# Chunked state-space scan and bilinear feed-forward on one core: one late store moved to GpSimd's queue, the state-decay spread as two 64-column products, two filler products fewer

## The chip, the cores and the metric

The kernel runs on one core of one Trainium2 chip. The metric is device time in microseconds (us), the median of several executions, lower is better. The profile is one further execution, recorded by the hardware profiler. PE is TensorE (matrix products; PEld are its weight loads), DVE is VectorE, ACT is ScalarE, POOL is GpSimd, SP is SyncE, which here only issues DMAs.

## The reference, cut to what matters

Two operators follow each other. The first is a chunked state-space scan over 4 batches, 8 heads and 768 steps, with head size 32 and state size 16:

```
cum = cumsum(log a)                      # within a chunk
M[i,j] = (C_i . B_j) * exp(cum_i - cum_j)   for i >= j
y[i]   = sum_j M[i,j] x_j  +  exp(cum_i) * C_i . state
state  = exp(sum log a) * state + sum_j exp(cum_last - cum_j) B_j x_j
```

The heads of `y` are then put side by side (3072 tokens of width 256) and go through the second operator, `((y @ w_a) * (y @ w_b)) @ w_out` with `d_ff` = 1536. Inputs and output are float32.

## The kernel before, in words

Sequences are cut into 6 blocks of 128 steps (`NBLK`), and the 4 batches into 2 pairs (`NBP`), which makes 12 pairs `p` of (block, two batches). For a pair the kernel scales B and C by running decays (`scale_bc`), turns them (on PE with `transposes` for the first four pairs, by a DMA transpose, `turn`, for the others), multiplies them (`scores`, into the PSUM tiles `SC`), multiplies by the causal mask (`mask`, mostly on DVE, at times on ACT and POOL), scales x (`scale_x`, L287 when on ACT), and forms y (`pv` with `pv_u`, L433; `outputs` for later pairs). The per-block decay of the state, one number for each head and block, is computed by POOL on 32 partitions (`hsx`, L795), spread to 128 partitions by a product with an indicator matrix (`gps`, L815), and copied by ACT to `G` (L818); `state_sums` multiplies by it.

The feed-forward part takes y in units. A unit is one "up" product pair, `aps` with `Wa` and `bps` with `Wb` (L601 for the first four pairs, `unit_mm`; L667 for blocks, `bunit`), an ACT copy of `aps` (`asb`, L615) and a DVE product with `bps` (L622 or L679). `out_mm` (L637) and `bout` (L694) multiply by `Wo`, ACT or DVE scales the result into `osb` (L706, L704), and a DMA stores it. `bout(blk, c, parts)` does a block's quarter `c`; the last one, `bout(5, 3, 2)`, is done in two halves, one stored from SP's queue and one from ACT's.

The order of the work on each engine is written out by hand: the kernel runs under a manual schedule, and each engine executes its instructions in the order of the program. Semaphore waits are put in by the framework. PSUM work tiles come from four banks, taken in the order of a written-out string (`BANKS`); a new tile in a bank waits until the last reader of the old tile is done. By that string `gps` has the bank of an `aps` tile, and the decay-factor tile behind it (`fps`, made by `factors(3, NBLK, ...)`, L248) has the bank of the tile `bps` of unit (1, 1), whose reader is DVE's product L622.

Two things at the edges matter here. Early on, PE has filler products (`warmup(n, bank)`, L220, on a zeroed tile) between real work; those at L775 stand behind the transposes of pair 1 and ahead of the first up products:

```
transposes(1, apart=True)
...
warmup(2, tcp)
aps = [unit_mm(0, 0, Wa), unit_mm(0, 1, Wa)]
asb = [evac_a(aps[0])]
scores(1)
```

And at the end, the DMAs of SP and ACT take turns on eight completion semaphores, in program order over both queues, and those of POOL on eight others. SP closes the program with a row of records (L1039) in which it waits for each of the sixteen, two at a time, from the first hardware one to the eighth, and then enters the barrier of all engines.

Of the kernel before, what the change touches and what calls it, by code (L numbers as in the profile page):

```python
# [28 lines left out]
def kernel(  # L29
# [13 lines left out]
    nc = tc.nc  # L43

    nb, H, S, D = x.shape
    N = B.shape[-1]
    Q = 128
    NBLK = S // Q
# [7 lines left out]
    NG = NBLK - 1  # L56
# [21 lines left out]
    indm = c32[:, 0:128]  # L78
# [26 lines left out]
    hsx = big.tile([BH, nb, NG], f32, name="hsx")  # L105
# [21 lines left out]
    def bank(name):  # L127
        return psf.tile([128, 512], f32, name=name, tag=f"ff{next(banks)}")
# [89 lines left out]
    def warmup(n, bank, cols=512):  # L218
        for _ in range(n):
            nc.tensor.matmul(  # L220
                bank[:, 0:cols], warm[:, 0:128], warm[:, 0:cols], start=True, stop=True, skip_group_check=True
            )
# [9 lines left out]
    def sel_over_mid(lo, hi, eng):  # L232
        eng.tensor_tensor(
            out=selr[:, lo:hi].rearrange("p k t c -> p k (t c)"),
            in0=sel.rearrange("p t b h -> p (t b h)").unsqueeze(1).broadcast_to((BH, hi - lo, 2 * NBP * H)),
            in1=rmid[:, lo:hi].unsqueeze(2).broadcast_to((BH, hi - lo, 2 * NBP * H)),
            op=ALU.mult,
        )
# [357 lines left out]
    def unit_mm(p, k2, W):  # L596
        ps = bank("aps" if W is Wa else "bps")
        for kk in range(2):
            k = 2 * k2 + kk
            for f in range(2):  # L600
                nc.tensor.matmul(  # L601
                    ps[:, kk * 2 * Q : (kk + 1) * 2 * Q],
                    W[k // 6][:, f, k % 6 // 3 * 384 : (k % 6 // 3 + 1) * 384].rearrange("p (c kk) -> p kk c", kk=3)[
                        :, k % 3
                    ],
                    X2T[:, p, :, f],
                    start=(f == 0),
                    stop=(f == 1),
                    skip_group_check=True,
                )  # L610
        return ps
# [73 lines left out]
    def bout(blk, c, parts=1):  # L685
        bt, j = divmod(c, NBP)
        hk = st[("FF", blk)]["hk"]
        rows = out[(2 * j + bt) * S + blk * Q :][0:Q]
        w = d_model // parts
        for part in range(parts):  # L690
            o_ps = bank("ops")
            cs = slice(part * w, part * w + w)
            for k in range(NK):
                nc.tensor.matmul(  # L694
                    o_ps[:, 0:w],
                    hk[:, k, c * Q : (c + 1) * Q],
                    Wo[:, k, cs],
                    start=(k == 0),
                    stop=(k == NK - 1),
                    skip_group_check=True,  # L700
                )
            o_sb = outp.tile([128, d_model], f32, name="osb", tag="osb")
            if parts > 1 and part == 0:
                nc.vector.tensor_scalar(o_sb[:, 0:w], o_ps[:, 0:w], 1.0 / (YS * YS), None, ALU.mult)  # L704
            else:
                nc.scalar.activation(out=o_sb[:, 0:w], in_=o_ps[:, 0:w], func=AF.Copy, scale=1.0 / (YS * YS))  # L706
            (nc.sync, nc.scalar)[part].dma_start(rows[:, cs], o_sb[:, 0:w])

    def loads_bc(p):
        if p < NP:  # L710
# [31 lines left out]
    tb, tcp = bank("tb"), bank("tc")  # L742
# [29 lines left out]
    scan(5, NBLK)  # L772
    over_mid(1, NBLK)
    sel_over_mid(1, NBLK, nc.vector)
    warmup(2, tcp)  # L775
    aps = [unit_mm(0, 0, Wa), unit_mm(0, 1, Wa)]
    asb = [evac_a(aps[0])]
    scores(1)
# [29 lines left out]
    for k2 in range(1, 3):  # L808
# [3 lines left out]
    scale_bc(2, 1, nc.gpsimd)  # L812
    go((1, 0), (1, 1), (1, 2))
    gps = bank("gps")
    nc.tensor.matmul(  # L815
        gps[:, 0 : nb * NG], indm, hsx.rearrange("p b g -> p (b g)"), start=True, stop=True, skip_group_check=True
    )
    nc.scalar.copy(G.rearrange("p b g -> p (b g)"), gps[:, 0 : nb * NG])  # L818
    factors(3, NBLK, bank("fps"))
    state_sums(0)  # L820
# [149 lines left out]
    masked(7, (0, 1, 2), *bu(2, 5, 6, 7, 8, 9, 10, 11))  # L970
    group(3)
    bout(2, 0)
    bout(2, 1)

    stage(8, True, (6, 7))
# [7 lines left out]
    for blk in range(4, NBLK):  # L983
        pB = blk * NBP + 1
        stage(pB, False)
        if blk > 4:
            prep_x(pB)
        loads_x(pB + 2, nc.sync)
        prep(pB + 2)
        masked(pB, (0, 1))  # L990
        bout(blk - 2, 2)
        masked(pB, (2, 3), *bu(blk - 1, 6, 7, 8, 9))
        group(blk)
        bout(blk - 2, 3)
        bgo(blk - 1, 10, 11)
        if blk + 1 < NBLK:
            stage(pB + 1, False, (pB - 1, pB))
            prep_x(pB + 1)
            masked(pB + 1, (0, 1))
            bout(blk - 1, 0)  # L1000
            masked(pB + 1, (2,))
            bout(blk - 1, 1)
            masked(pB + 1, (3,), *bu(blk, 0, 1, 2, 3, 4, 5))
# [40 lines left out]
```

## Time and profile before

| what | value |
|---|---|
| runs (3) | 124.07, 124.44, 124.65 us; median 124.44 us |
| the profiled execution's own time | 123.91 us |
| its span (first to last instruction) | 122.2 us |
| busy share: PE, DVE, ACT, POOL | 96%, 70%, 58%, 51% |
| the chain that ended last, by engine | PE 93%, ACT 1%, POOL 1%, DVE 1% |
| granted TensorE clock | 1.0 |

The span is the time between the first and the last recorded instruction; what lies around it is 1.7 us in this execution. Busy shares are averages over the span. The chain of work that ended last is followed back from the last instruction; a line on it is work that nothing else hid, as far as the profile shows.

### The profile page before, as it was taken

How to read it: one execution, taken by the hardware profiler on the slowest of the kernel's cores; microseconds unless marked ns; L12 is line 12 of the kernel's file. 1: busy time of each engine (PE TensorE's matmuls, PEld its weight loads, DVE VectorE, ACT ScalarE, POOL GpSimd, SP SyncE). 2: the span in 40 equal slices, each digit the busy share in tenths (PEclk: the TensorE clock that was granted, in tenths of full speed). 3: DMA queues.
4: the chain of work that ended last, by engine and by line, in shares of the span. 5: the costliest groups of instructions: out<-in, count | busy, mean ns of one | idle time of the engine just before them, and what ended most of it. 6: DMA issues, size and time to landing. Idle time of an engine off the chain costs nothing.

```text
span 122.2 us, 3713 instructions
## 1 busy us (share of the span) xinstructions
PE 117.1 (96%) x1455; PEld 80.1 (66%) x1455; DVE 85.9 (70%) x163; ACT 71.4 (58%) x141; POOL 61.9 (51%) x107
## 2 busy tenths in 40 slices
PE   5999999999999999999999999999999999999990
PEld 2446789978898898644476464766465684645880
DVE  1877897795969599499984999667799435748000
ACT  0367756866466477887668637745645737575230
POOL 7999998966953876099921993147400000000000
PEclk9999999999999999999999999999999999999999
DMA  3999999998969999799789854879501012010131
GB/s 64 165 167 240 152 215 155 218 143 83 95 95 131 150 104 155 76 134 148 55 143 128 200 187 127 96 102 160 161 0 51 16 45 68 0 48 0 43 117 55
DMA packets 66737, 13.73 MB, mean 112 GB/s; under 512 B 61616, under 2 KB 66384, under 8 KB 66720
## 3 DMA queue, kind: packets, MB, share of 16 engines
q1 hardware_dynamic: 62592, 9.53, 49.8%
q0 software_dynamic: 2128, 3.61, 16.8%
q10 hardware_dynamic: 2000, 0.36, 1.6%
q8 instruction: 11, 0.18, 0.7%
q14 instruction: 6, 0.05, 0.1%
HBM read 11.13 MB, written 3.15 MB: 117 GB/s over the span
## 4 chain that ended last, share of the span: by engine, by line
PE 93%; ACT 1%; issue 1%; POOL 1%; DVE 1%; POOLq 0%
PE ops L694 18%; PE aps L667 17%; PE bps L667 17%; PE aps L601 9%; PE ops L637 9%; PE bps L601 9%; PE SC L220 3%; PE SC L358 2%; PE SC L419 2%; PE SC L373 1%; PE SC L433 1%; PE SC L508 1%; PE fps L260 1%; POOL bm L304 1%; ACT bt L337 1%
## 5 line engine op out<-in xcount | busy, mean ns | idle before, releaser
L615 ACT COPY asb<-aps 128x512 f32<-128x512 f32 x72 | 42.0, 586 | 14.3 <-PE aps L667 9.6
L679 DVE TENSOR_TENSOR hkb<-bps,asb 128x512 f16<-128x512 f32 x48 | 32.4, 689 | 12.6 <-ACT asb L615 11.4
L667 PE MATMUL aps<-XB,Wa 128*128 128x512 f16 x96 | 28.6, 379 | 0.0
L667 PE MATMUL bps<-XB,Wb 128*128 128x512 f16 x96 | 28.5, 379 | 0.0
L694 PE MATMUL ops<-Wo,hkb 128*128 128x256 f16 (+1 forms) x204 | 22.5, 267 | 0.0
L694 PEld LDWEIGHTS <-hkb 128*128 128x128 f16 x204 | 18.5, 98 | 3.1
L413 DVE TENSOR_TENSOR t<-SC,causal_q 128x512 f16<-128x512 f32 x27 | 17.3, 682 | 3.3 <-PE SC L358 3.3
L622 DVE TENSOR_TENSOR hk<-bps,asb 128x512 f16<-128x512 f32 x24 | 16.2, 684 | 4.1 <-ACT asb L615 3.7
L667 PEld LDWEIGHTS <-Wb 128*128 128x128 f16 x96 | 9.9, 103 | 10.9
L667 PEld LDWEIGHTS <-Wa 128*128 128x128 f16 x96 | 9.7, 103 | 9.1 <-issue 0.2
L601 PE MATMUL aps<-X2T,Wa 128*128 128x256 f16 x96 | 14.3, 274 | 0.2 <-DVE X2T L493 0.2
L706 ACT ACTIVATE osb<-ops 128x256 f32<-128x256 f32 (+1 forms) x16 | 6.0, 377 | 14.3 <-PE ops L694 14.2
L601 PE MATMUL bps<-X2T,Wb 128*128 128x256 f16 x96 | 14.1, 273 | 0.0
L411 POOL TENSOR_TENSOR t<-tmp,causal_q 128x512 f16<-128x512 f32 x5 | 5.8, 1161 | 11.7 <-ACT tmp L410 11.6
L289 POOL TENSOR_SCALAR x<-xn 128x512 f16<-128x512 f32 x7 | 10.4, 1490 | 2.1 <-DMA xn<-in_x_dram 1.8
L637 PE MATMUL ops<-Wo,hk 128*128 128x256 f16 x96 | 11.3, 273 | 0.0
L601 PEld LDWEIGHTS <-Wa 128*128 128x128 f16 x96 | 9.4, 103 | 1.3 <-DVE X2T L493 0.3
L601 PEld LDWEIGHTS <-Wb 128*128 128x128 f16 x96 | 9.8, 103 | 0.6
L637 PEld LDWEIGHTS <-hk 128*128 128x128 f16 x96 | 9.0, 98 | 1.3
L413 DVE TENSOR_TENSOR t<-SC,causal 128x512 f16<-128x512 f32 x13 | 8.2, 684 | 0.9 <-PE SC L373 0.8
L304 POOL TENSOR_TENSOR bm<-bn,fB 128x256 f16<-128x256 f32 x11 | 7.1, 642 | 2.5 <-DMA bn<-in_B_dram 1.7
L296 POOL TENSOR_TENSOR planes<-cn,fC 128x256 f16<-128x256 f32 x8 | 5.0, 620 | 4.7 <-DMA cn<-in_C_dram 4.5
(94 smaller groups left out, 117.0 us busy)
## 6 DMA issues: line engine op xcount, KB each, us to landing
out_dram<-osb SPq DMA_DIRECT2D x23, 128.0 KB, 1.8
xn<-in_x_dram SPq DMA_DIRECT2D x7, 256.0 KB, 4.2
cn<-in_C_dram SPq DMA_DIRECT2D x8, 128.0 KB, 3.9
bn<-in_B_dram SPq DMA_DIRECT2D x8, 128.0 KB, 4.5
Wa<-in_moe_w_a_dram POOLq DMA_DIRECT2D x2, 384.0 KB, 5.9
Wb<-in_moe_w_b_dram POOLq DMA_DIRECT2D x2, 384.0 KB, 7.3
Wo<-in_moe_w_out_dram POOLq DMA_DIRECT2D x2, 384.0 KB, 6.7
xn<-in_x_dram POOLq DMA_DIRECT2D x4, 128.0 KB, 6.5
```

What stands on the lines that cost most here:

```text
L289: eng.tensor_scalar(xo, xi, XS, None, ALU.mult)
L304: eng.tensor_tensor(out=m_, in0=raw, in1=(f[:, blk, :, bp] if factor is None else factor).unsqueeze(3).broadcast_to((128, 2, H, N)), op=AL ...
L411: nc.gpsimd.tensor_tensor(out=o_, in0=tmp, in1=c_, op=ALU.mult)
L413: nc.vector.tensor_tensor(out=o_, in0=i_, in1=c_, op=ALU.mult)
L601: nc.tensor.matmul(ps[:, kk * 2 * Q : (kk + 1) * 2 * Q], W[k // 6][:, f, k % 6 // 3 * 384 : (k % 6 // 3 + 1) * 384].rearrange("p (c kk) -> ...
L615: (nc.vector.tensor_copy if on_dve else nc.scalar.copy)(asb, a_ps)
L622: nc.vector.tensor_tensor(out=s["hk"][:, 2 * k2 : 2 * k2 + 2, :].rearrange("p k q -> p (k q)"), in0=b_ps, in1=asb, op=ALU.mult)
L637: nc.tensor.matmul(o_ps[:, 0:d_model], hk[:, k, bt * Q : (bt + 1) * Q], Wo[:, k, :], start=(k == 0), stop=(k == NK - 1), skip_group_check= ...
L667: nc.tensor.matmul(t_, W[k // 6][:, f, k % 6 // 3 * 384 : (k % 6 // 3 + 1) * 384].rearrange("p (c kk) -> p kk c", kk=3)[:, k % 3], XB[:, b ...
L679: return lambda: nc.vector.tensor_tensor(out=s["hk"][:, k], in0=ps[1], in1=asb, op=ALU.mult)
L694: nc.tensor.matmul(o_ps[:, 0:w], hk[:, k, c * Q : (c + 1) * Q], Wo[:, k, cs], start=(k == 0), stop=(k == NK - 1), skip_group_check=True,)
L706: nc.scalar.activation(out=o_sb[:, 0:w], in_=o_ps[:, 0:w], func=AF.Copy, scale=1.0 / (YS * YS))
```

## The change

Three edits. The store of `bout(4, 3)` is issued from GpSimd's queue instead of SP's. The spread of the state decays is written as two products of 64 columns each (the two halves of the array's columns) instead of one of 128. The two fillers at L775 are left out.

```diff
-            (nc.sync, nc.scalar)[part].dma_start(rows[:, cs], o_sb[:, 0:w])
+            eng = nc.gpsimd if (blk, c) == (NBLK - 2, 3) else (nc.sync, nc.scalar)[part]
+            eng.dma_start(rows[:, cs], o_sb[:, 0:w])
...
     sel_over_mid(1, NBLK, nc.vector)
-    warmup(2, tcp)
     aps = [unit_mm(0, 0, Wa), unit_mm(0, 1, Wa)]
...
     gps = bank("gps")
-    nc.tensor.matmul(
-        gps[:, 0 : nb * NG], indm, hsx.rearrange("p b g -> p (b g)"), start=True, stop=True, skip_group_check=True
-    )
+    for c0 in (0, 64):
+        nc.tensor.matmul(
+            gps[c0 : c0 + 64, 0 : nb * NG],
+            indm[:, c0 : c0 + 64],
+            hsx.rearrange("p b g -> p (b g)"),
+            start=True,
+            stop=True,
+            skip_group_check=True,
+            tile_position=(0, c0),
+        )
```

The order on every engine is otherwise as before: on PE two fillers are gone and one product has become two, on SP one store is gone, and on POOL one store stands behind the last scaling of x.

## The prediction

> **What bounds the kernel.** I read the chain that ended last first. It is PE for 93% of the span, with POOL, DVE and ACT at 1% each, so a piece of PE's chain that goes is worth its length until something that isn't PE comes late instead. The chain around the two early edits:
>
> ```profile
> 10.25 0.40 PE SC L326 x4
> 10.65 0.43 PE tc L220 x2
> 11.08 0.87 PE aps L601 x8
> 11.95 0.36 PE SC L373 x32
> ...
> 13.34 1.42 PE bps L601 x12
> 14.76 0.44 PE SC L433 x32
> ...
> 18.07 0.44 PE bps L601 x4
> 18.51 0.32 PE gps L815 x2
> 18.83 0.47 PE fps L248 x12
> ```
>
> (start, length, what, in us). The fillers are 0.43 us of the chain, the spread `gps` 0.32 us. So at most 0.43 us comes from the one edit, and from the other 0.32 us less what its replacement takes. Then the timeline, for what PE waits for close behind them:
>
> ```profile
> 10.69 0.84 ACT L337 ACTIVATE bt<-SC,ch 128x256 f16<-128x256 f16 x2 [0.35 <-PE SC L326]
> 11.88 0.27 PEld L373 LDWEIGHTS <-bt 32*64 32x64 f16 x32 [0.20 <-issue]
> 13.98 0.66 ACT L287 ACTIVATE x<-xn 128x512 f16<-128x512 f32 x1
> 14.70 0.24 PEld L433 LDWEIGHTS <-x 64*32 64x32 f16 x32 [0.21 <-ACT x L287]
> 17.89 1.52 DVE L622 TENSOR_TENSOR hk<-bps,asb 128x512 f16<-128x512 f32 x2 [0.23 <-ACT asb L615]
> 18.76 0.43 PEld L248 LDWEIGHTS fps<-selr,Pr 32*64 32x64 f32 x12
> ```
>
> Each of these three PE steps has another engine's work just ahead of it: the copies `bt`, the scaled x, and DVE's product L622. Last the end of the program, in the waits of SP's queue, the DMA issues and the source view of its closing records:
>
> ```profile
> SPq L1039 <- DMA out_dram<-osb: 1.8, 1, 1.8
> ```
>
> ```profile
> out_dram<-osb ACTq DMA_DIRECT2D x1, 64.0 KB, 1.6
> ```
>
> ```profile
> L1039 SPq EVENT_SEMAPHORE  x11: 17/28/28, 119.0 to 122.1; - x11
> ```
>
> SP waits 1.8 us for one last store, ACT's half of the last quarter, which takes 1.6 us from its issue at 119.26, to 120.85. In the trace's single records SP's closing row goes: first record at 118.98, then the one for the first hardware semaphore at 120.87, and seven more at 120.93, 120.99, 121.06, 121.11, 121.18, 121.24 and 121.30, that is one every 0.061 us. All those other stores had landed by 120.15. SP enters the end at 121.36, 0.51 us after the last landing, of which 0.43 us are seven checks of things long done.
>
> **The change, part by part.**
>
> *Fillers (L775).* Removed: 2 products, 0.43 us. Needed for the up products at once: `Wa` (landed at 10.27) and the y of pair 0 (the last DVE copy starts at 10.17 and takes 0.29, so 10.46). The transposes' last product starts at 10.43, so the up products can start near 10.49 instead of 10.92. Behind them `scores(1)` writes the PSUM tile that both copies `bt` read, and those are bound to the transposes, not to the fillers: 10.69 + 0.84 = 11.53, and 0.04 from an end to PE's start (the hand-over read from `x`, below). It starts at 11.57 instead of 11.88: **0.31 us** are left of 0.43. Next cover: `pv(1)` started at 14.70 right behind ACT's scaled x (13.98 + 0.66 = 14.65, then 0.04 to PE). That step isn't bound to PE alone. Its input, the second half of x of pair 1, landed at 13.71, and ACT's record of the wait for it is at 13.73. ACT's queue ahead of it moves up by the 0.31, to be ready near 13.68, and then waits for the landing; 13.73 plus 0.06 (from such a record to its instruction, as in other rows of ACT) is 13.79, plus 0.64 (632 to 663 ns in the five rows of L287) and 0.05, so PE starts `pv(1)` near 14.49. **0.21 us** are left; the ends are 0 (the landing comes later in an unprofiled run) and 0.31 (earlier). The masks end earlier than that: DVE's follow the scores, and POOL's, held by DMA issues until 13.04, ends by 14.27.
>
> *Spread of decays (L815).* The product is two records of 32x128 weights in float32, 0.13 us apart, and the next product starts 0.32 after the first. The new shape is nearest to L248 and L260, products of 32 rows by 64 columns in float32: a product of those is two records 0.007 apart, the next follows after 0.058, or 0.07 to 0.08 for the first of a row (0.47 for 6 products in the chain above). Two products are 0.14, and the edit alone is worth 0.32 - 0.14 = 0.18 us. But `fps` behind it needs its bank from DVE's L622 of unit (1, 1), which ends 0.16 us ahead of `fps`'s weight load at 18.76 in the single records (18.60) and needs 0.04 to hand over. So it can move by no more than 0.12 beyond what DVE itself moves, and DVE moves with PE: **0.12 us**, ends 0 and 0.18. The Trainium skill (TensorE: Matmul & The Clock Gate, LDWEIGHTS) has the weight load go with the number of columns alone, so that two loads of 64 take as long as one of 128. By that, this term would be 0.
>
> *How far it travels.* PE is then 0.33 us ahead. I looked at each landing close to a PE use: `Wb`'s second half lands at 19.03, its use is at 19.58 and would be at 19.25; the turned tile of pair 5 lands at 41.61, its use is at 42.17, then 41.84; other turned tiles have 2 us and more, x of pair 2 (25.80) has cover until pair 2's `pv` at 27.2. None comes late at 0.33; the nearest would at about 0.5. Waits of PE for ACT and DVE further on go back to PE's own products. So I keep 0.33, with an end of 0.1 (only the spread travels).
>
> *The store.* It leaves SP's queue, where nothing stood behind it: SP is idle ahead of each of the last stores, and issues one in 0.33. POOL has had no work since 87 us, so it queues nothing either. What moves is the turn of the semaphores. Counted from the DMA issues, SP and ACT issue 73 DMAs, so the last one (ACT's half) has the first semaphore, and after the change, as the 72nd, the eighth. SP's closing row then spends its seven checks while the last store is under way, and ends 0.08 instead of 0.51 after the landing: **0.43 us** = 7 x 0.061. Ends: 0 if that row isn't what the end waits for, 0.43 else. The barrier behind it is the same. The POOL store itself must land before 120.4; from its data at 113.7 that leaves 6.7 us. The Trainium skill (DMA: Bandwidth & Descriptors, Issuing engines are not separate DMA queues) has another issuing engine save only the sequencer's issue time. By that, this term would be 0, since SP's 0.33 is hidden.
>
> **Sum.** 0.21 + 0.12 + 0.43 = 0.76, rounded to 0.75 us, off the profiled execution's 123.91: 123.16, with a span of 121.45. That execution is 0.53 under the median of 124.44; the saving is the same for both, so 123.69.
>
> **The rivals.**
>
> *The front doesn't travel.* A landing (x of pair 1, then `Wb`) or a bank holds PE where it was, and 0 to 0.12 is left of 0.33. For it: PE's step at 14.70 is already within 0.3 of a landing. Against: after 19.6 no landing is closer than 0.5. Time: 124.44 - 0.43 - 0.06, near 123.95.
>
> *The end gives nothing.* The closing row runs beside something else, such as other engines' drains, or moving the store has only SP's 0.33 of issue to save, which is hidden. For it: no view puts the row on the chain. Against: the barrier's records of all other engines start after SP's last. Time: 124.44 - 0.33 = 124.11. This is what the Trainium skill's section on issuing engines, named above, leads to.
>
> *The whole of the front is had*, 0.43 + 0.18, and the end: 124.44 - 1.04 = 123.4. It needs the landing 0.25 earlier and the copies `bt` out of the way, which rows speak against.
>
> *Two half products take as long as one*, 0.16 each, everything else as forecast: 124.44 - 0.64 = 123.80. The 0.007 between the records of the 64-column shape, against 0.13, speaks against it. This is what the Trainium skill's section on LDWEIGHTS, named above, leads to.
>
> *The POOL store lands late* (slower). POOL's DMAs take 4.7 to 7.3 us in the median from issue to landing by the DMA issues, the longest 8.1 for `Wb`. SP's own store of the same 128 KB takes 1.8. It decides from 6.7 us on. At 8.1 it lands at 121.9, four checks (0.24) are behind it, and SP ends 1.6 later than forecast: 125.3. Against: those rows are from stretches in which the DMA engines were 0.7 to 0.9 busy, and here they are 0.5 at most.
>
> *The clock falls without the fillers* (slower). The first 8 fillers took 2.96 us for 3328 columns, five later ones 1.25 for 2560, so PE was at about half speed until 6.3 us. If it fell back for as long (1.2 to 6.3 us), half of 5 us would be lost: near 126.2. Against: without the fillers PE idles 0.1 us, and it stayed fast over the 0.23 that its weight loads waited for POOL ahead of 10.25.
>
> **Chances.** Forecast 0.51; front doesn't travel 0.22; end gives nothing 0.09; whole front 0.07; half products equal 0.04; late store 0.04; clock 0.03. Faster by over 0.5% (0.62 us, about what a measurement of this kernel can tell from no change) are the forecast, the whole front and, just, the equal halves, 0.62; two points go to "same", since the forecast stands only 0.13 beyond the bound: 0.60. Same: 0.22 + 0.09 + 0.02 = 0.33. Slower: 0.07. The range reaches from 123.3 (the whole front) to 124.2 (end gives nothing), which leaves out the slower cases and some spread of the runs (124.07 to 124.65 before).
>
> **What would show it.** Right: the up products start near 10.5 and `scores(1)` near 11.57; `pv(1)` near 14.49 behind ACT's x; the two `gps` products take 0.14, and `fps` starts near 18.43; from there every PE piece is 0.33 earlier; SP's closing row has its long wait in its last record and ends within 0.1 of the last landing. Wrong: PE pieces after 20 us that stand where they stood, a closing row with its wait in the middle (the POOL store's), or filler-free up products further apart than 0.109 us.

## The result, and the profile after

| | before | changed | ratio, 95% interval |
|---|---|---|---|
| first comparison | 124.35 us (17 runs) | 123.79 us (17 runs) | 0.995 [0.9931, 0.997] |
| second comparison | 124.29 us (17 runs) | 123.83 us (12 runs) | 0.9971 [0.9949, 0.9992] |

The changed kernel is faster by 0.62 us by the first ratio (0.37 to 0.86 by its interval, on 124.4) and by 0.36 by the second (0.10 to 0.63). The forecast of 123.69 is 0.10 and 0.14 below the medians; the saving that was forecast, 0.75, lies inside the first interval and above the second.

The execution of the changed kernel that was profiled first took 127.15 us, because an early load came 1.5 us late and a stretch ran at half clock (below); the ratios leave it out, and with it one execution of each kernel in the second comparison (125.49 and 127.97 us). The lines here are from a later execution of the same kernel, at 123.59 us with a span of 121.9, against 123.91 and 122.2 before.

The chain that ended last, in order of time (start, length, what, in us):

```profile
7.26 6.90 DMA xn<-in_x_dram
14.16 0.02 issue
14.18 0.02 ACTq L287
14.20 0.04 issue
14.24 0.64 ACT x L287
14.88 0.04 issue
14.92 0.50 PE SC L433 x32
...
18.73 0.22 PE gps L816 x4
18.95 0.45 PE fps L248 x12
```

Before, this chain was PE from 10.25 on, but for one step of DVE (0.43 at 15.22). Now a DMA stands in it: the second half of x of pair 1, which lands at 14.16 and holds ACT's scaled x and PE's `pv(1)` behind it. The spread `gps` is 0.22 instead of 0.32. The same stretch in the timeline:

```profile
10.64 0.78 PEld L601 LDWEIGHTS <-Wa 128*128 128x128 f16 x8 [0.18 <-DMA Wa<-in_moe_w_a_dram]
...
11.63 0.27 PEld L373 LDWEIGHTS <-bt 32*64 32x64 f16 x32 [0.21 <-ACT bt L337]
...
14.24 0.63 ACT L287 ACTIVATE x<-xn 128x512 f16<-128x512 f32 x1 [0.37 <-DMA xn<-in_x_dram]
14.92 0.24 PEld L433 LDWEIGHTS <-x 64*32 64x32 f16 x32 [0.69 <-ACT x L287]
...
18.66 0.19 PEld L816 LDWEIGHTS gps<-hsx,c 32*64 32x64 f32 x4 [0.21 <-issue]
...
18.86 0.42 PEld L248 LDWEIGHTS fps<-selr,Pr 32*64 32x64 f32 x12
```

The first up products start 0.27 earlier than before (10.65 against 10.92) and `scores(1)` 0.25 earlier (11.63 against 11.88), but `pv(1)` 0.22 later (14.92 against 14.70). From `gps` to `fps` it is 0.205 in the single records against 0.323, which brings the lateness down to 0.11, and with that PE goes through to its last product (118.81 against 118.70). So the front of this execution lost 0.11, and its saving of 0.32 is what the end gave, 0.43, less that. In SP's waits and in the DMA issues:

```profile
SPq L1046 <- DMA out_dram<-osb: 1.4, 3, 0.7
```

```profile
out_dram<-osb SPq DMA_DIRECT2D x22, 128.0 KB, 1.8
...
out_dram<-osb POOLq DMA_DIRECT2D x1, 128.0 KB, 2.1
```

SP's closing row now waits three times, 1.4 us in all and 0.7 at the longest, instead of once for 1.8: it meets the last three stores in the order in which they land. The POOL store took 2.1 us and landed at 116.58, 4.4 before the last one. Time of SP's closing records after the last landing, from the trace's single records (row: the completion semaphore that the record waits for; "end" is SP's entry into the barrier):

```
                      before  eight on POOL  two on POOL  store alone  changed
landed at, us         120.85      121.63        122.13       120.88     120.97
semaphore 1            0.017       0.017        earlier      earlier    earlier
semaphore 2            0.079       0.079        earlier      earlier    earlier
semaphores 3 to 6   0.14-0.33   0.14-0.33       earlier      earlier    earlier
semaphore 7            0.385       0.385         0.016       earlier    earlier
semaphore 8            0.446       0.446         0.078        0.017      0.017
end                    0.511       0.511         0.143        0.082      0.082
```

The three columns between are experiments of the next section.

### The profile page after: what moved, and what is told of

It is laid out like the page before. It is cut to its first block, busy times and chain, and to the rows that moved or that the text cites. A ratio compares the mean times of both kernels' runs of the same rounds, so it can differ in the third digit from the quotient of the medians.

```text
span 125.4 us, 3712 instructions
## 1 busy us (share of the span) xinstructions
PE 119.4 (95%) x1455; PEld 80.9 (64%) x1455; DVE 85.9 (68%) x163; ACT 71.4 (57%) x141; POOL 62.5 (50%) x108
## 4 chain that ended last, share of the span: by engine, by line
PE 88%; DMA 5%; POOL 3%; issue 0%; DVE 0%; ACT 0%; POOLq 0%
PE ops L694 17%; PE aps L667 17%; PE bps L667 17%; PE aps L601 10%; PE bps L601 9%; PE ops L637 9%; DMA Wa<-in_moe_w_a_dram 5%; PE SC L358 2%; PE SC L419 2%; POOL cn L148 1%; PE SC L373 1%; PE SC L433 1%; PE SC L508 1%; POOL bn L148 1%; POOL causal L208 1%; PE fps L248 1%
## 5 line engine op out<-in xcount | busy, mean ns | idle before, releaser
L615 ACT COPY asb<-aps 128x512 f32<-128x512 f32 x72 | 42.0, 585 | 15.5 <-PE aps L667 9.7
L667 PE MATMUL aps<-XB,Wa 128*128 128x512 f16 x96 | 28.6, 379 | 0.0
L667 PE MATMUL bps<-XB,Wb 128*128 128x512 f16 x96 | 28.5, 379 | 0.0
L622 DVE TENSOR_TENSOR hk<-bps,asb 128x512 f16<-128x512 f32 x24 | 16.1, 683 | 4.7 <-ACT asb L615 3.5
L667 PEld LDWEIGHTS <-Wb 128*128 128x128 f16 x96 | 9.9, 103 | 10.9
L601 PE MATMUL aps<-X2T,Wa 128*128 128x256 f16 x96 | 15.3, 287 | 1.6 <-DMA Wa<-in_moe_w_a_dram 1.3
L667 PEld LDWEIGHTS <-Wa 128*128 128x128 f16 x96 | 9.7, 103 | 9.1 <-issue 0.2
L601 PE MATMUL bps<-X2T,Wb 128*128 128x256 f16 x96 | 15.3, 291 | 0.0
L708 POOL DMA_DIRECT2D out_dram<-osb x1 | 0.6, 639 | 27.4 <-ACT osb L706 27.4
L601 PEld LDWEIGHTS <-Wb 128*128 128x128 f16 x96 | 10.3, 108 | 1.2
```

Source lines behind the costliest of these rows:

```text
L601: nc.tensor.matmul(ps[:, kk * 2 * Q : (kk + 1) * 2 * Q], W[k // 6][:, f, k % 6 // 3 * 384 : (k % 6 // 3 + 1) * 384].rearrange("p (c kk) -> ...
L615: (nc.vector.tensor_copy if on_dve else nc.scalar.copy)(asb, a_ps)
L622: nc.vector.tensor_tensor(out=s["hk"][:, 2 * k2 : 2 * k2 + 2, :].rearrange("p k q -> p (k q)"), in0=b_ps, in1=asb, op=ALU.mult)
L667: nc.tensor.matmul(t_, W[k // 6][:, f, k % 6 // 3 * 384 : (k % 6 // 3 + 1) * 384].rearrange("p (c kk) -> p kk c", kk=3)[:, k % 3], XB[:, b ...
```

## The experiments

**Theory** (the prediction's): the end gives 0.43, by the place of the last store among the eight semaphores alone; the spread 0.12; the fillers 0.21. **Rivals**: the end gives nothing, or gives because SP is relieved of a store, whatever the order; the front doesn't travel, since a landing holds PE.

**The store alone.** Only the first hunk of the diff.

> The kernel before with the one store moved to GpSimd's queue and nothing else. Theory of the closing row (the last store's semaphore moves from the first to the eighth place, so that SP's seven other checks run while that store is under way): 0.43 us less than before, ratio 0.9965; in the trace SP's long wait is in its ninth closing record, and its drain starts about 0.08 after the last landing (0.51 before). Rival, by which another issuing queue saves only the issue time, which is hidden: no change, ratio 1.000, and the drain still about 0.5 after the last landing. Rival, late store: SP's wait sits in the fifth closing record (the one with GpSimd's third semaphore), and the time is over that of before.

Measured: 124.25 us, ratio 0.9974 [0.9948, 0.9999], that is -0.32 us (-0.65 to -0.01). In SP's waits:

```profile
SPq L1040 <- DMA out_dram<-osb: 1.4, 3, 0.7
```

This is the changed kernel's row, with the fillers in place and the spread undivided: the end belongs to the store. By the table its closing row ends 0.082 after the landing instead of 0.511.

**Eight late stores on POOL's queue.** SP is relieved of eight stores, but the last store has the first semaphore again, since eight fewer of SP and ACT take turns.

```diff
-            (nc.sync, nc.scalar)[part].dma_start(rows[:, cs], o_sb[:, 0:w])
+            eng = nc.gpsimd if (blk, c) in ((3, 2), (3, 3), (4, 0), (4, 1), (4, 2), (4, 3), (5, 0), (5, 1)) else ...
+            eng.dma_start(rows[:, cs], o_sb[:, 0:w])
```

> The kernel before with eight late stores moved to GpSimd's queue: those of bout(3, 2) and (3, 3), all four of bout(4, .), and (5, 0) and (5, 1). SP and ACT then issue 65 DMAs, so the last one has the first semaphore again, as before the change. Theory of the closing row: nothing is gained, ratio 1.000; SP's long wait is in its second closing record and its drain starts about 0.5 after the last landing, although SP is relieved of eight stores. Rival, by which taking stores off SP's queue is what helped: at least the gain of the single store, ratio 0.997 or less.

Measured: 124.43 us, ratio 1.0008 [0.9984, 1.0033]: no gain. In SP's waits:

```profile
SPq L1040 <- DMA out_dram<-osb: 1.8, 1, 1.8
```

One wait for 1.8 us, as before the change, and by the table seven checks behind it, 0.061 apart. Relieving SP is worth nothing; the turn of the semaphores is.

**Two late stores on POOL's queue**, `(4, 2)` and `(4, 3)`, which leaves the last store the seventh semaphore.

> The kernel before with two late stores moved to GpSimd's queue, bout(4, 2) and (4, 3). SP and ACT issue 71 DMAs, so the last store has the seventh semaphore. Theory of the closing row: the long wait is in the eighth closing record, one more check of 0.06 follows, and the drain starts 0.14 after the last landing (0.51 in the kernel before, 0.08 with one store moved). Rival, fewer stores on SP are what helps: the drain starts as early as with one store or earlier.

Measured in one profile: the end 0.143 after the landing, one check (0.061) more than with one store moved, as expected. Its 124.83 us are no verdict on the end: `Wa` landed at 11.59, and the up products started 0.72 later than before.

**The spread alone.** Only the third hunk.

> The kernel before with the spread of decays as two 64-column products and nothing else. Theory: the product behind it starts 0.20 after the first gps record (0.32 before) because its bank is free only when DVE's product of unit (1, 1) is done; 0.12 us less in all, ratio 0.999, too little to be told from 1 by the times alone. Rival, the products' own length decides: 0.14 from the first gps record to the next product, 0.18 us less. Rival, two half loads take as long as one: 0.32, no change.

Measured: 124.25 us, ratio 0.9978 [0.9953, 1.0002], -0.27 us with an interval from -0.58 to +0.02, which holds the 0.12 and also nothing. The tile's rows show the size of the step better:

```profile
L816 PEld LDWEIGHTS gps<-hsx,c x4: 127/130/131, 18.7 to 18.7; 32*64 32x64 f32 x4
L816 PE MATMUL gps<-hsx,c x4: 207/218/228, 18.7 to 18.7; 32*64 32x20 f32 x4
```

(the changed kernel's; duration min/median/max in ns, first and last start, forms.) The four records start at 18.660, 18.667, 18.740 and 18.746: 0.007 inside a product and 0.08 for a product, as forecast, against 0.132 between the two records of the undivided one. `fps` follows 0.205 or 0.206 after the first in all seven profiles with the two products, in those at an early front and in those at a late one, and 0.323 in all seven with one. By its semaphore, DVE's L622 ends 0.04 ahead of `fps` with two products (18.82 to 18.86), the length of a hand-over, where it ended 0.16 ahead before (18.60 to 18.76): the bank is what holds `fps` now.

**The fillers alone.** Only the line `warmup(2, tcp)` is left out.

> The kernel before without the two fillers ahead of the first up product and nothing else. Theory of the forecast: scores of pair 1 start 0.31 earlier, pv of pair 1 is held by the landing of x of pair 1 and starts 0.21 earlier, and 0.21 us are left at the end, ratio 0.998. Rival, landings in other executions are as late as in the profiled execution of the changed kernel (first half of Wa at 11.8 instead of 10.3): in such an execution the up products wait for Wa, nothing is gained or the clock drops to half for a stretch of about 7 us, and the time is 2 to 4 us over that of before; if that were common, the ratio would be over 1.

Measured: 124.40 us, ratio 0.9998 [0.9978, 1.0019]: -0.02 us (-0.27 to +0.24), so the 0.21 is near the edge of the interval, and nothing in its middle. The timeline:

```profile
10.44 0.78 PEld L601 LDWEIGHTS <-Wa 128*128 128x128 f16 x8
...
14.01 0.63 ACT L287 ACTIVATE x<-xn 128x512 f16<-128x512 f32 x1 [0.27 <-DMA xn<-in_x_dram]
...
14.69 0.24 PEld L433 LDWEIGHTS <-x 64*32 64x32 f16 x32 [0.58 <-ACT x L287]
14.69 0.42 PE L433 MATMUL SC<-t,x 64*32 64x128 f16 x32 [0.31 <-ACT x L287]
```

The up products start at 10.44, 0.47 earlier than before and as early as forecast, `scores(1)` at 11.50, and PE then stands 0.31 ahead of `pv(1)`, which starts at 14.69 where it was 14.70. The whole gain is eaten at one place, by x of pair 1, which lands at 13.92 here.

**The store and the spread, fillers kept.** The change without its second hunk.

> The changed kernel with its two fillers put back: store moved and spread split. Theory of the forecast: 0.43 + 0.12 = 0.55 us less than before, ratio 0.9956, and 0.21 more than the changed kernel. Rival, the fillers' removal brings nothing on the whole (the landing of x of pair 1 or of Wa binds): the same as the changed kernel, 123.8, with no execution in which the clock drops while PE waits for Wa, or with a shorter drop, since the fillers hold PE busy for 0.43 of that wait.

Measured: 123.75 us, ratio 0.9963 [0.9941, 0.9984]. That is not told apart from the changed kernel's 0.995 and 0.9971. The single parts multiply to the whole: 0.9974 x 0.9978 x 0.9998 = 0.9950.

**x of pair 1 not waited for, without and with the fillers.** In both, the scaled x of pair 1 is made from the x of pair 0, which landed long before, so the y of pair 1 is not the reference's and only the times count; the first also leaves out the fillers.

```diff
-        xo, xi = ..., pair_in[p][2].rearrange("p h r d -> p (h r d)")
+        xo, xi = ..., pair_in[0 if p == 1 else p][2].rearrange("p h r d -> p (h r d)")
```

> The kernel before without the fillers, where the scaled x of pair 1 is made from the x of pair 0, which has landed long before (the loads stay as they are; y of pair 1 is not the reference's). ACT then has no landing to wait for ahead of pv of pair 1. Theory, by which the landing of x of pair 1 ate the gain of the fillers' removal: the scaled x starts about 0.3 earlier than in the twin with fillers, pv of pair 1 too (near 14.4 in an execution whose first half of Wa lands by 10.4), and the time is 0.3 us under the twin's. Rival, something else behind it holds PE (the banks, DVE or the weights' second half): pv starts earlier, but the up products of the next units or the first block stand where they stood, and the time is the twin's.

> The twin with the fillers kept: the kernel before, with the scaled x of pair 1 made from the x of pair 0 (y of pair 1 is not the reference's). Theory: with the fillers ACT's own queue reaches that step only at about 13.98, so nothing changes against the kernel before when x lands by 13.9: ratio 1.000, or up to 0.1 us less where it lands later. Rival: the landing was already late before the change, and the time falls by 0.2 us or more.

Measured: 124.03 us, 0.9978 [0.9957, 1.0] without fillers, and 124.04 us, 0.9998 [0.9977, 1.002] with them: equal medians, ratios 0.002 apart with intervals that overlap. The 0.3 us between them that was expected did not show, and the two do not decide the question. The timeline of the one without fillers shows why the gain is small even so:

```profile
10.82 0.78 PEld L601 LDWEIGHTS <-Wa 128*128 128x128 f16 x8 [0.42 <-DMA Wa<-in_moe_w_a_dram]
...
14.62 0.42 PE L433 MATMUL SC<-t,x 64*32 64x128 f16 x32
...
15.85 0.24 PE L460 MATMUL SC<-x,bm 64*32 64x64 f16 x13 [0.63 <-issue]
```

With x out of the way the up products waited for `Wa`, which landed at 10.78, and then PE stood for 0.63 in the middle of the 32 products of L460, with nothing that it waited for.

**The changed kernel with the same edit.**

> The changed kernel, where the scaled x of pair 1 is made from the x of pair 0 (y of pair 1 is not the reference's), so that ACT waits for no landing there. Theory: if the first half of Wa lands by 10.4, pv of pair 1 starts at about 14.4 (14.7 in the kernel before) and fps near 18.35 (18.76), with the span 0.8 to 0.9 under that of before (121.3); if Wa lands later, the up products start 0.05 behind it and all of that is later by as much. Rival: pv starts at 14.4 and the first block's products at 51.0 as before.

Measured in one profiled execution: 125.72 us. `Wa` landed at 11.10, and in the chain:

```profile
15.36 0.18 PE SC L460 x19
15.54 2.35 issue
17.89 0.24 PE SC L460 x13
```

It is the same place, after 19 products of L460, and now 2.35 us long. The DMA view shows a queue of instructions at work there. In the window from 15 to 16 us of this kernel:

```profile
q8 instruction: 1, 0.02, 6.0%
```

(packets, MB, share of the engines.) By the trace's single packets, the first 16 KB of this queue in the kernel come at 15.70 and end at 16.66, and PE goes on 1.23 later. In the other 13 profiles this packet starts between 12.51 and 13.25 and ends between 13.64 and 14.74. Counted over PE's recorded products, the place is ahead of the 223rd in all seven profiles that show it: after 19 products of L460 without the two fillers, after 17 with them. The other seven reached it 1.49 or more after the packet's end and show no pause. From the start of the 222nd product to that of the 223rd, 0.01 us without a pause, it is 0.06 in the changed kernel, 0.09 with the fillers out, 0.20 before the change, 0.52 with the store alone, 0.60 in the kernel with fillers and x not waited for, and 0.82 and 2.55 in the two kernels shown last. No profile has PE past it earlier than 1.22 after the packet's end; where PE stood there, it went on 1.22 to 1.46 after it. That is the picture of PE waiting for its code, and no more than that: it is read from 14 profiles, and no run moved the load.

**x of pair 1 from SP's queue.** The changed kernel, with that load issued from SP's queue instead of from the end of POOL's, and two more late stores on POOL's, so that the last store keeps the eighth semaphore.

```diff
     nc.sync.dma_start(c32, p32_t.ap())
+    for bt in range(2):
+        load1(nc.sync, 1, 2, bt)
...
     load_w(0)
-    for bt in range(2):
-        load1(nc.gpsimd, 1, 2, bt)
...
-            eng = nc.gpsimd if (blk, c) == (NBLK - 2, 3) else ...
+            eng = nc.gpsimd if (blk, c) in ((NBLK - 2, 1), (NBLK - 2, 2), (NBLK - 2, 3)) else ...
```

> The changed kernel with both halves of x of pair 1 loaded from SP's queue, behind its last early load, instead of GpSimd's behind the weights; two more late stores go to GpSimd's queue, bout(4, 1) and (4, 2), so that the last store keeps the eighth semaphore. Theory: x of pair 1 lands well before 13.6, pv of pair 1 starts 0.2 to 0.3 earlier than in the changed kernel, and the time is up to 0.3 us under it, 0.6 to 0.9 under the kernel before. Rival, the early transfers only share one bandwidth: what x gains the halves of Wa and Wb lose (they land 0.3 or more later), the up products wait for them, and the time is that of the changed kernel or above.

Measured: 123.62 us, ratio 0.9948 [0.9932, 0.9964], not told apart from the changed kernel's 0.995. In the timeline:

```profile
10.84 0.78 PEld L601 LDWEIGHTS <-Wa 128*128 128x128 f16 x8 [0.37 <-DMA Wa<-in_moe_w_a_dram]
...
13.94 0.66 ACT L287 ACTIVATE x<-xn 128x512 f16<-128x512 f32 x1
...
14.71 0.24 PEld L433 LDWEIGHTS <-x 64*32 64x32 f16 x32 [0.20 <-ACT x L287]
```

ACT no longer waits for a landing, and `pv(1)` still starts at 14.71: `Wa` landed at 10.80 in this execution, so the fillers' place was idle anyway. Whether the earlier load of x made `Wa` late is open, since 10.80 lies inside the 10.24 to 11.79 of the other profiles.

**The changed kernel again**, first for a profile alone, then timed and profiled.

> The changed kernel once more, for a profile of an execution in which the clock does not drop. Theory: the last store's wait is in SP's last closing record and the drain starts 0.08 after the last landing; the first product behind gps starts 0.20 after the first gps record; the up products start at the landing of the first half of Wa plus 0.05, or at 10.45 if it lands by 10.4, and pv of pair 1 starts 0.75 to 0.8 after the landing of the second half of x of pair 1, or 0.1 behind PE's own bps products if Wa landed late.

> The changed kernel a third time, timed, to see how often its clock drops and to have a profile with an early landing of Wa. Theory: the ratio is 0.995 as before; in an execution with the first half of Wa landed by 10.5 the up products start near 10.5, pv of pair 1 starts 0.75 to 0.8 behind the landing of the second half of x of pair 1 and so at 14.6 to 14.8, fps 0.20 behind the first gps record, and the span is 0.5 to 0.6 under that of before. Rival, by which the removal of the fillers makes the clock drop in a good part of the executions: granted clock of 0.975 or less and 126 us or more in three or more of the timed executions.

Measured: the second of them is the comparison and the profile of the section above. The first took 126.92 us. In its timeline and on its page:

```profile
11.82 1.11 PE L601 MATMUL aps<-X2T,Wa 128*128 128x256 f16 x8 [1.28 <-DMA Wa<-in_moe_w_a_dram]
```

```profile
PEclk9999558999999999999999999999999999999999
```

`Wa` landed at 11.78, PE stood for 1.28 us, and 0.87 after it went on, the granted clock fell to half from 12.69 to 19.52. The execution profiled first was the same: landing 11.79, half clock from 12.23 to 19.06. The first block's products (L667) started at 54.44 instead of 51.10; 1.18 of these 3.33 are the later start of the up products; the rest, 2.15, came about over the stretch at half clock. In the 27 executions of the changed kernel that were timed without a profile the clock was at 0.997 or above. Of the kernels with fillers, two profiles had `Wa` nearly as late (11.57 and 11.59), PE stood 0.64 and 0.56 in them, and the clock stayed. Two against two is too little to show that fillers are what kept it, and other executions speak against it. With the fillers in place, six timed executions had a mean granted clock of 0.986 or 0.987 (three of the kernel before, at 126.74, 127.97 and 129.44 us, two of the store alone and one of the store and the spread), and one more of the store alone had 0.66, at 171.93 us; with the fillers alone taken out it was two, 0.986 and 0.982. Nor does the length of one stand decide: PE stood 1.48 us ahead of `pv(1)` in the profile of the spread alone and 2.35 us in the kernel further above, and the clock stayed at full.

## Why the prediction was right, point by point

**The store: right, 0.43.** The end after the last landing went from 0.511 to 0.082, 0.429, with the store alone and with the whole change alike, and two and eight moved stores gave the ends that the turn of the semaphores asks for. The rival "the end gives nothing" is out, and with it the use that was made of the Trainium skill (DMA: Bandwidth & Descriptors, Issuing engines are not separate DMA queues). By that section this term would be 0. What it says of transfers is not contradicted (2.1 us on POOL's queue, 1.8 on SP's), but the gain here came from neither transfer nor issue.

**The spread: right, 0.12.** 0.323 to 0.205 is 0.118, bounded by DVE's reader of `fps`'s bank as the prediction had it. The timed runs alone could not have shown it. That it travels is seen where the front is otherwise as before: with x from SP's queue the up products of pair 1 start at 15.72 (15.70 before), `fps` at 18.65 (18.76), and PE's last product at 118.59 (118.70). The rival of two equal halves is out: a half took 0.08, not 0.16. It went back to the Trainium skill (TensorE: Matmul & The Clock Gate, LDWEIGHTS), whose rule by the number of columns gives no equal halves for these float32 products. The step from one weight load to the next does halve with the columns (0.108 for 128, 0.055 for 64), but the undivided product is two loads one behind the other, while the second load of a half starts 0.007 after its first.

**The fillers: the mis-sized term, 0.21 in the sum, about 0 in the runs.** The rule of the step was right: from the landing of x to `pv(1)` it was to take 0.78, and took 0.77 (13.92 to 14.69) and 0.76 (14.16 to 14.92). Wrong was the landing. The prediction took 13.71 from the one execution it had, gave 0 as an end for a later one, and then held 0.21 to be the likeliest. `fps` was to start near 18.43 and every PE piece behind it 0.33 earlier; in the profile shown `fps` starts at 18.86 and the pieces are 0.11 later. The prediction itself had named pieces that don't move up as a sign of being wrong. A gain needs x by 14.70 - 0.77 = 13.93 and `Wa` by 10.9, where the fillers end. Over 14 profiles, of all kernels, `Wa`'s first half landed between 10.24 and 11.79, in seven of them after 10.9, and, where it stayed on POOL's queue, x 3.1 to 3.8 later (once 4.6); the 10.27 and 13.71 of the profile before are at the early end. What held the start of pair 1's up products (15.70 before), in some of the profiles:

| kernel | `Wa` landed | x landed | instruction packet's end | up products of pair 1 start | held by |
|---|---|---|---|---|---|
| before | 10.27 | 13.71 | 14.05 | 15.70 | ACT's x and PE's own products, both just done |
| fillers out | 10.40 | 13.92 | 13.96 | 15.69 | x |
| changed | 10.60 | 14.16 | 14.14 | 15.93 | x |
| x from SP's queue | 10.80 | not waited for | 13.64 | 15.72 | `Wa` |
| fillers out, x not waited for | 10.78 | not used | 14.39 | 16.03 | the stop ahead of the 223rd product, 1.46 after the packet |
| store alone | 10.28 | 13.89 | 14.16 | 15.75 | the stop ahead of the 223rd product, 1.41 after the packet |

That is the rival "the front doesn't travel" for the filler's part of the front, with two more holders than it named: `Wa`, and the stop that looks like a wait for code. With the term at 0 the sum is 0.43 + 0.12 = 0.55, between the measured 0.62 and 0.36 and inside both intervals. That the forecast of 0.75 still lies inside the first interval is luck as far as these 0.21 go: the interval is wider than the term. That the timed executions were held in the same way is inferred from the profiles, since landings can't be read without one.

**The rest.** Beyond 20 us nothing came late, as said: from the first L667 product to PE's last it took 67.71 before and 67.70 after. The late POOL store didn't happen (2.1 us of the 6.7 it had). The fall of the clock happened in two profiles, by another way than the rival's: not the 0.1 of idle time that the fillers' absence leaves, but that plus a late load; its size was forecast as 2.5 and was 2.15. The whole front was never had.

## What to carry to other kernels

Look at what the end of the program does after the last landing: if a row of checks in a fixed order stands there, the last transfer to land should be the last that is checked, and moving one unrelated DMA to another queue may be enough. Work that covers the arrival of a load is worth its length only in executions where the load is early; before pricing its removal, take the landing from several executions, and add up every other thing that arrives at about that time, perhaps the engine's code too. A gain of 0.1 us is read from the records at its place, not from medians that agree to 0.3%.

## What the runs showed of the hardware that was not expected

- In seven of 14 profiles PE stopped ahead of the same recorded product, the 223rd, until 1.22 to 1.46 us after a 16 KB packet of the instruction queue had ended, whether that held nothing up (0.20 between two starts, before the change) or left PE idle for 2.35 us. The packet itself took 0.96 to 1.66 us among the other transfers.
- The same early load landed between 10.24 and 11.79 us in different executions.
- The granted clock fell to half, for 6.83 us each time, in the two profiles in which PE had stood for 1.3 us ahead of the first up products, and stayed at full in two others in which PE stood for 1.48 and 2.35 us at about 15.5. No run shows what decides.
- The closing records of SP cost 0.061 us each even when what they check was done long before.
